# Three x tiles loaded by two DMA queues at once, and parameter loads moved behind ScalarE's table load

## The chip, the cores and the metric

The kernel runs on one core of a Trainium2 chip. The metric is device time in microseconds (us) of one execution.

Engine names in the profile: PE is TensorE (matmul), PEld its weight loads, DVE is VectorE, ACT is ScalarE, POOL is GpSimd, SP is SyncE. A "q" behind a name (SPq, ACTq) is the engine's sequencer; a row such as "SPq ... DMA_DIRECT2D" is the time in which that sequencer *issues* a DMA, not the time in which the data move. PE's results land in a memory called PSUM (`ps`), which the kernel uses in banks.

## The reference, cut to what matters

The input x has 2048 tokens of 1024 features. It is normalised, and three terms are added.

```python
xn = layernorm(x)                       # per token, over 1024 features
return x + A_ref(xn, ...) + B_ref(xn, w1, b1, w2)
# A_ref: a diagonal complex recurrence over the tokens, with projections B (in) and C (out)
# B_ref: (xn @ w1 + b1) -> h * tanh(softplus(h)) -> @ w2, with 3584 hidden features
```

Only the opening matters: before the first real matmul can run, a tile of x must arrive, be normalised and be transposed, and the first columns of w1 must be there.

## The kernel before

Tokens are worked in four blocks of 512, each of four tiles of 128 tokens. The steady part is matmuls end to end. The opening, which the change touches, loads the four x tiles of block 0, the first seven slots of a weight ring and four small parameter vectors. Cuts are marked `# ...`.

```python
for h in range(2):                                   # x tile 0, two column halves, 128 rows x 1 KB
    SP.dma(lambda e, h=h: e.dma_start(xx[:, 0, 0, h * 512:(h + 1) * 512], A_x[0, 0:P, h * 512:(h + 1) * 512]),
           DmaSem(nc, "d_x00_%d" % h), writes=[b_xx[0][0].parts[h]])
for q in (1, 3):
    load_x(SP, 0, q)                                 # x tiles 1 and 3, 128 rows x 2 KB
for src, r0, n in ((A_log_dt, 2 * NJ, NJ), (A_Lambda_im, NJ, NJ), (A_Lambda_re, 0, NJ),
                   (B_b1, 3 * NJ, NF)):              # 8, 8, 8 and 28 rows of 256 B
    AC.dma(lambda e, src=src, r0=r0, n=n: e.dma_start(
        st[r0:r0 + n, :], src.rearrange("(j p) -> j p", p=P)), s_st, writes=[b_st])
# ...
for i in range(NRING):                               # weight slots, 512 KB each
    ring_load()                                      # on SP
    if i == 0:
        load_x(SP, 0, 2)
# ...
keep_busy(36)                                        # filler matmuls, ahead of real work
aop(lambda e: e.activation(rs[:, :, 3], ..., AF.Sqrt), ...)   # its table load comes first on ScalarE
for q in range(2):
    first_sums_v(q, 0); first_sums_v(q, 1)           # VectorE statistics
    first_var_v(q)
    first_sqrt(q)                                    # ScalarE
keep_busy(14, [b_mv[0]])
PE.op(lambda e: e.transpose(ps16(2)[:, 0:NST], st[:, :], ident[0:NST, 0:NST]),   # the parameter block
      reads=[b_st, b_ident], writes=[b_ps[2]])
keep_busy(8, [b_mv[1]])
first_apply(0); first_transpose(0)                   # x tile 0 normalised (VectorE), transposed (PE)
first_apply(1, 2); first_transpose(1)
keep_busy(8)
# ... copies of the transposed tiles to SBUF, then the copy of the parameter block
for f in range(4):
    first_half(f, 0, 0, NK // 2)                     # first w1 matmuls, 256 tokens wide
```

In the profile of before, line L477 is the filler, L393 the transposes of x, L523 the 256-wide w1 matmuls and L665 the full-width (512) ones. In the changed kernel the same lines are L485, L401, L532 and L674.

## Time and profile before

| | before |
|---|---|
| median of 3 runs (lowest to highest) | 621.22 us (621.11 to 621.61) |
| span of the profiled run, granted clock | 620.0 us, 1.0 |
| PE busy | 616.7 us |
| first w1 matmuls / first full-width w1 matmuls start (timeline / chain) | 8.73 / 18.72 us |

First the page's busy times (each with its share of the span and its number of instructions):

```profile
PE 616.7 (99%) x2961; PEld 287.2 (46%) x2961; DVE 462.4 (75%) x677; ACT 247.6 (40%) x161; POOL 50.6 (8%) x47
```

Then the chain of waits of before: the work that ended last, followed back. The columns are start, duration (us) and what it was.

```profile
0.79 2.23 DMA xx<-in_A_x_dram
...
3.04 0.71 DVE stats L351
...
6.52 0.62 PE ps L477 x8
7.14 1.23 PE ps L393 x16
8.38 0.45 PE ps L477 x8
8.82 3.24 PE ps L523 x28
...
13.39 5.33 PE ps L523 x48
18.72 39.71 PE ps L665 x184
```

From 6.52 us on the chain is PE to 617.9 us, 0.4 us before the end. Whatever delays the start of the full-width matmuls at 18.72 us delays the end of the kernel by the same amount.

The timeline of before, opening only: start, duration, engine, line, what; in brackets the idle time in front and what ended it.

```profile
0.79 0.88 SPq L291 DMA_DIRECT2D xx<-in_A_x_dram  x2
0.79 0.59 ACTq L297 DMA_DIRECT2D st<-in_A_log_dt_dram  x1
...
1.72 0.92 SPq L287 DMA_DIRECT2D xx<-in_A_x_dram  x2
...
2.68 0.44 SPq L321 DMA_DIRECT2D ring<-in_B_w_dram  x1
3.04 1.50 DVE L351 BATCH_NORM_STATS2 stats<-xx 128x6 f32<-128x512 bf16 x2 [2.06 <-DMA xx<-in_A_x_dram]
...
6.29 0.19 PE L488 MATMUL ps<-ident,st 52*128 52x52 bf16 x1
...
10.57 1.21 PEld L523 LDWEIGHTS ps<-xnT,ring 128*128 128x128 bf16 x12 [0.21 <-DMA ring<-in_B_w_dram]
```

### The profile page before, as it was taken

What the parts mean: (1) busy time and instruction counts of PE and PEld (TensorE: products, weight loads), DVE (VectorE), ACT (ScalarE), POOL (GpSimd) and SP (SyncE); (2) the same over time, 40 slices, a digit from 0 to 9 for tenths busy, and PEclk for the clock granted to TensorE, in tenths of its full rate; (3) what the DMA queues carried; (4) which work ended last, traced back from release to release, by engine and by line L of the source; (5) the groups of instructions that cost most, each with busy time, mean ns of one, the idle gap of its engine ahead of it and who ended that gap; (6) DMA issues with size and microseconds to landing.
All of it is one profiled execution on the core that took longest, in us unless ns stands there. A gap on an engine that the chain in (4) does not pass through costs nothing.

```text
span 620.0 us, 7386 instructions
## 1 busy us (share of the span) xinstructions
PE 616.7 (99%) x2961; PEld 287.2 (46%) x2961; DVE 462.4 (75%) x677; ACT 247.6 (40%) x161; POOL 50.6 (8%) x47
## 2 busy tenths in 40 slices
PE   9999999999999999999999999999999999999998
PEld 7544444444444444444444444444444444444444
DVE  7897999999467599998147659999624856999603
ACT  5689996440079940000008992000001999000000
POOL 1998000000100000000010000000000000000000
PEclk9999999999999999999999999999999999999999
DMA  8999956840364301783054430276203542033001
GB/s 282 255 294 248 220 111 190 218 136 0 124 204 147 135 1 36 205 197 107 17 187 135 150 122 1 85 204 174 82 35 104 169 167 69 1 122 117 1 0 69
DMA packets 95804, 79.41 MB, mean 128 GB/s; under 512 B 48922, under 2 KB 78234, under 8 KB 95770
## 3 DMA queue, kind: packets, MB, share of 16 engines
q1 hardware_dynamic: 92272, 71.64, 42.1%
q10 hardware_dynamic: 2538, 4.14, 1.8%
q0 software_dynamic: 960, 3.15, 1.6%
q8 instruction: 24, 0.39, 0.3%
q14 instruction: 10, 0.08, 0.0%
HBM read 63.19 MB, written 4.19 MB: 109 GB/s over the span
## 4 chain that ended last, share of the span: by engine, by line
PE 99%; DVE 1%; DMA 0%; issue 0%; DVEq 0%
PE ps L744 49%; PE ps L665 30%; PE ps L686 18%; PE ps L523 1%; DVE stats L351 0%; DMA xx<-in_A_x_dram 0%; PE ps L393 0%; PE ps L758 0%; PE ps L477 0%; DVE xx L812 0%; DVE mv L356 0%; DVE rs L377 0%; DVEq L131 0%
## 5 line engine op out<-in xcount | busy, mean ns | idle before, releaser
L744 PE MATMUL ps<-ring,act 128*128 128x512 bf16 x896 | 194.0, 379 | 0.0
L665 PE MATMUL ps<-xnT,ring 128*128 128x512 bf16 x856 | 185.4, 379 | 0.0
L644 ACT ACTIVATE act<-hb 128x3584 bf16<-128x3584 bf16 x16 | 50.9, 3183 | 224.1 <-DVE hb L673 224.0
L744 PEld LDWEIGHTS ps<-ring,act 128*128 128x128 bf16 x896 | 87.7, 98 | 105.7
L665 PEld LDWEIGHTS ps<-xnT,ring 128*128 128x128 bf16 x856 | 83.7, 98 | 100.8
L673 DVE TENSOR_SCALAR hb<-ps,par 128x512 bf16<-128x512 f32 x112 | 82.4, 747 | 56.0 <-PE ps L665 54.8
L686 PE MATMUL ps<-xnT,BT 128*128 128x512 bf16 x512 | 111.2, 379 | 0.0
L744 PE MATMUL ps<-CT,hT 128*128 128x512 bf16 x506 | 109.9, 379 | 0.0
L691 DVE TENSOR_TENSOR mt<-ps,tab 128x1024 bf16<-128x1024 f32 x64 | 75.4, 1219 | 17.5 <-PE ps L686 16.6
L686 PEld LDWEIGHTS ps<-xnT,BT 128*128 128x128 bf16 x512 | 50.1, 98 | 60.4
L744 PEld LDWEIGHTS ps<-CT,hT 128*128 128x128 bf16 x506 | 49.5, 98 | 59.7
L709 DVE TENSOR_TENSOR_SCAN hT<-cs,qi,hT 128x512 bf16<-128x512 f32 x48 | 58.9, 1269 | 0.0
L789 DVE TENSOR_TENSOR xx<-ps,xx 128x1024 bf16<-128x1024 f32 (+1 forms) x16 | 18.8, 1190 | 46.0 <-PE ps L744 45.9
L645 ACT ACTIVATE act<-act 128x3584 bf16<-128x3584 bf16 x16 | 51.0, 3190 | 0.2
L646 ACT ACTIVATE act<-act 128x3584 bf16<-128x3584 bf16 x16 | 51.0, 3190 | 0.2
L714 DVE TENSOR_TENSOR mt<-hT,tab 128x1024 bf16<-128x1024 bf16 x64 | 41.4, 688 | 1.1
L651 DVE TENSOR_TENSOR act<-act,hb 128x3584 bf16<-128x3584 bf16 x16 | 32.3, 2017 | 1.3 <-ACT act L646 1.3
L287 POOL DMA_DIRECT2D xx<-in_A_x_dram x12 | 6.7, 559 | 253.2 <-DVE xx L789 247.9
L620 ACT ACTIVATE ct<-CT,cs 128x512 f32<-128x512 bf16 x16 | 11.5, 720 | 26.7 <-DVE CT L622 25.9
L645 ACT ACT_TABLE_LOAD x16 | 20.5, 1283 | 0.3
L646 ACT ACT_TABLE_LOAD x16 | 20.5, 1283 | 0.3
L709 DVE TENSOR_TENSOR_SCAN hT<-cs,hT 128x512 bf16<-128x512 f32 x16 | 18.7, 1209 | 0.0
(86 smaller groups left out, 276.7 us busy)
## 6 DMA issues: line engine op xcount, KB each, us to landing
ring<-in_B_w_dram SPq DMA_DIRECT2D x112, 512.0 KB, 4.1
out_dram<-xx ACTq DMA_DIRECT2D x15, 256.0 KB, 2.1
xx<-in_A_x_dram POOLq DMA_DIRECT2D x12, 256.0 KB, 3.5
xx<-in_A_x_dram SPq DMA_DIRECT2D x3, 256.0 KB, 3.7
xx<-in_A_x_dram SPq DMA_DIRECT2D x2, 128.0 KB, 2.2
dsk<-in_A_Dskip_dram SPq DMA_DIRECT2D x1, 256.0 KB, 8.2
xnT<-xn SPq DMA_TRANSPOSE x12, 4.6
BT<-in_A_B_re_dram SPq DMA_TRANSPOSE x8, 6.2
```

The source lines that it names most:

```text
L644: aop(lambda e: e.activation(a, hs, AF.Exp), reads=[b_hb[g % 2]], writes=[b_act[g]])
L645: aop(lambda e: e.activation(a, a, AF.Ln, bias=1.0), reads=[b_act[g]], writes=[b_act[g]])
L646: aop(lambda e: e.activation(a, a, AF.Tanh), reads=[b_act[g]], writes=[b_act[g]])
L651: vop(lambda e: e.tensor_tensor(a, a, hs, op=ALU.mult), reads=[b_act[g], b_hb[g % 2]], writes=[b_act[g]])
L665: PE.mm(lambda e, k=k, w=w: e.matmul(ps[:, bank, :], lhsT=w, rhs=xnT[:, k, :], start=k == 0, stop=k == NK - 1), reads=[b_ring[s]] + b_xnT, ...
L673: vop(lambda e: e.tensor_scalar(hb[:, hs, :], ps[:, bank, :], b1(f), None, op0=ALU.add), reads=[b_ps[bank], b_par], writes=[b_hbf[hs]])
L686: PE.mm(lambda e, j=j, ci=ci, k=k, bank=bank: e.matmul(ps[:, bank + ci, :], lhsT=BT[:, ci, j, k, :], rhs=xnT[:, k, :], start=k == 0, stop= ...
L691: vop(lambda e, s=s, u=u, j=j: e.tensor_tensor(mt[:, s, :, :], u, tab[:, s, j, :].unsqueeze(1).to_broadcast([P, 2, TB]), op=ALU.mult), rea ...
L709: vop(lambda e, ci=ci, init=init: e.tensor_tensor_scan(out=hT[:, ci, j, :], data0=cj("r", j).to_broadcast([P, TB]), data1=hT[:, ci, j, :], ...
L714: vop(lambda e, s=s: e.tensor_tensor(mt[:, s, :, :], hT[:, :, j, :], tab[:, s, j, :].unsqueeze(1).to_broadcast([P, 2, TB]), op=ALU.mult), ...
L744: PE.mm(lambda e: e.matmul(ps[:, u, :], lhsT=lhsT, rhs=rhs, start=st_, stop=last), reads=reads, writes=[b_ps[u]], first=st_, last=last)
L789: vop(lambda e: e.tensor_tensor(xr, src, xr, op=ALU.add), reads=b_ps[bank:bank + n] + [b_x], writes=[b_x])
```

## The change

The intent: the halves of x tiles 0, 1 and 3 are issued by SyncE and ScalarE at the same time, 64 tokens each, so that x is out sooner; ScalarE's parameter loads make room for them and go behind its table load; PE takes the parameter block later, since the parameters come later. The core of the diff:

```diff
+    def load_both(q, lo, hi, sem, bufs):
+        for n, queue in enumerate((SP, AC)):
+            p0 = n * (P // 2)
+            queue.dma(lambda e, p0=p0: e.dma_start(xx[p0:p0 + P // 2, 0, q, lo:hi],
+                                                   A_x[0, q * P + p0:q * P + p0 + P // 2, lo:hi]), sem, writes=bufs)
+
     for h in range(2):
-        SP.dma(lambda e, h=h: e.dma_start(xx[:, 0, 0, h * 512:(h + 1) * 512], A_x[0, 0:P, h * 512:(h + 1) * 512]),
-               DmaSem(nc, "d_x00_%d" % h), writes=[b_xx[0][0].parts[h]])
+        load_both(0, h * 512, h * 512 + 512, DmaSem(nc, "d_x00_%d" % h, nper=2), [b_xx[0][0].parts[h]])
     for q in (1, 3):
-        load_x(SP, 0, q)
-    for src, r0, n in (... the four parameters ...):
-        AC.dma(...)
+        load_both(q, 0, D, DmaSem(nc, "d_x0%d_2" % q, nper=2), [b_xx[0][q]])
+
+    def load_parameters():
+        for src, r0, n in (... the four parameters ...):
+            AC.dma(...)
 # ...
     aop(lambda e: e.activation(rs[:, :, 3], ..., AF.Sqrt), ...)
+    load_parameters()
 # ...
     keep_busy(14, [b_mv[0]])
-    PE.op(lambda e: e.transpose(ps16(2)[:, 0:NST], st[:, :], ...), ...)
     keep_busy(8, [b_mv[1]])
     first_apply(0)
     first_transpose(0)
     first_apply(1, 2)
     first_transpose(1)
+    PE.op(lambda e: e.transpose(ps16(2)[:, 0:NST], st[:, :], ...), ...)
     keep_busy(8)
```

More of the change, by code (lines that the diff above doesn't have):

```diff
@@ L288, in load_x @@
                   s_xx[i][q] if blk else s_x0[q], writes=[b_xx[i][q]])
+    def load_both(q, lo, hi, sem, bufs):
[3 more added lines that the diff above has]
+                                                   A_x[0, q * P + p0:q * P + p0 + P // 2, lo:hi]), sem, writes=bufs)
     for h in range(2):
-        SP.dma(lambda e, h=h: e.dma_start(xx[:, 0, 0, h * 512:(h + 1) * 512], A_x[0, 0:P, h * 512:(h + 1) * 512]),
-               DmaSem(nc, "d_x00_%d" % h), writes=[b_xx[0][0].parts[h]])
+        load_both(0, h * 512, h * 512 + 512, DmaSem(nc, "d_x00_%d" % h, nper=2), [b_xx[0][0].parts[h]])
     for q in (1, 3):
-        load_x(SP, 0, q)
-    for src, r0, n in ((A_log_dt, 2 * NJ, NJ), (A_Lambda_im, NJ, NJ), (A_Lambda_re, 0, NJ),
-                       (B_b1, 3 * NJ, NF)):
-        AC.dma(lambda e, src=src, r0=r0, n=n: e.dma_start(
-            st[r0:r0 + n, :], src.rearrange("(j p) -> j p", p=P)), s_st, writes=[b_st])
+        load_both(q, 0, D, DmaSem(nc, "d_x0%d_2" % q, nper=2), [b_xx[0][q]])
+    def load_parameters():
+        for src, r0, n in ((A_log_dt, 2 * NJ, NJ), (A_Lambda_im, NJ, NJ), (A_Lambda_re, 0, NJ),
+                           (B_b1, 3 * NJ, NF)):
+            AC.dma(lambda e, src=src, r0=r0, n=n: e.dma_start(
+                st[r0:r0 + n, :], src.rearrange("(j p) -> j p", p=P)), s_st, writes=[b_st])
     items = []
@@ L487, in build_kernel @@
     keep_busy(14, [b_mv[0]])
-    PE.op(lambda e: e.transpose(ps16(2)[:, 0:NST], st[:, :], ident[0:NST, 0:NST]),
-          reads=[b_st, b_ident], writes=[b_ps[2]])
     keep_busy(8, [b_mv[1]])
@@ L494, in build_kernel @@
     first_transpose(1)
+    PE.op(lambda e: e.transpose(ps16(2)[:, 0:NST], st[:, :], ident[0:NST, 0:NST]),
+          reads=[b_st, b_ident], writes=[b_ps[2]])
     keep_busy(8)
```

## The prediction

> **What bounds the kernel now.** TensorE. The page gives PE 616.7 of 620.0 us busy, at full clock; the chain of waits is unbroken PE work from 6.52 us to 617.9 us. From 18.72 us on (the first full-width w1 matmuls) the change touches nothing: it can gain or lose only what moves that start.
>
> **The opening, read from the timeline and the chain.** The two halves of x tile 0 are issued at 0.79 and 1.26 us (0.41 us each on SyncE) and take 2.2 and 2.1 us to land. VectorE starts its statistics at 3.04 us and is busy until 6.46; tile 1 (issued 1.72, 3.1 us to landing) arrives at about 4.8, just when VectorE wants it. The transposes start at 7.13, the first w1 matmuls at 8.73. Two limits hide behind it: the weight load at 10.57 waited 0.21 us for the second w1 slot, and VectorE 0.34 us for x tile 2 until 9.05. Both are late in one saturated stream: the DMA share is 0.75 to 1.4 from 2.5 us on.
>
> **What the change does.**
> - The x0, x1, x3 bytes are the same and run on the same DMA engines. The Trainium skill ("DMA: Bandwidth & Descriptors", Rules for kernel authors) says that two transfers to disjoint partition halves share the engines and aren't worth it, and that a second issuing engine saves issue time only. The saturated stream fits.
> - Issue time: 128 rows cost 0.41 to 0.50 us, 8 rows 0.29 to 0.32 us; I estimate 0.35 us for 64 rows. SyncE reaches the first weight load about 0.3 us sooner. But ScalarE's first issue took 0.59 us, twice its later ones (0.29), so its half of x0 is probably out at 1.4 us, against 1.2 us for the same columns today. I expect x0 to land 0.2 us sooner to 0.2 us later. There is a dip to 152 GB/s at 3.0 to 3.5 us that a second queue may fill, worth up to 0.2 us for tile 1 and everything behind.
> - ScalarE: four x issues end near 2.6 us (parameters ended at 2.40), table load 1.28 us, then four parameter issues of 0.3 us: free at about 5.4 not 3.94. The first square root, at 4.82 now, moves to about 5.4. VectorE reads it only at 6.38: hidden.
> - Parameters should land at about 8 us (now before 6.28). PE now needs them after the transposes of tile 1, at about 8.2, ahead of the first w1 matmuls. Tight.
>
> **Sum.** Gain 0 to 0.4 us from earlier x and weights, loss 0 to 0.5 us from late parameters and the transposed block moved onto the path (0.06 to 0.19 us). I predict 621.0 us, 8 in 10 between 620.2 and 622.1. Chance of faster by over 2% 0.005, within 2% 0.99, slower 0.005.
>
> **What would show it.** The start of the first w1 matmuls (8.73 now) and of the full-width ones (18.72 now, predicted 18.3 to 18.9); x0's landing near 3.0; the second w1 slot's landing; ScalarE's first issue again near 0.6 us; PE's wait for the parameter tile under 0.5 us.
>
> **What would make it wrong.** SyncE's weight issues take 5.6 us for five from 3.71 us: held back. If ScalarE's parameter issues are too, the square roots and everything behind slip by 1 to 2 us. Or parameters land after 9 us and PE stands. Or both queues together fill the stream sooner than I think, for a gain of 0.5 us or more.

## More of the kernel before

SyncE needs 1.85 us for its four x issues, and the first weight slot is issued at 2.68 us. The parameter block is transposed at 6.29 us without a wait: the parameters were there (the raw trace has the last of them landed at 4.84 us).

## The result, and the profile after

| | before | after |
|---|---|---|
| median of 6 runs (lowest to highest) | 621.29 us (621.11 to 621.61) | 623.72 us (622.41 to 624.28) |
| span of the profiled run, granted clock | 620.0 us, 1.0 | 622.4 us, 1.0 |
| PE busy | 616.7 us | 616.7 us |
| first full-width w1 matmuls | 18.72 us | 21.15 us |

The ratio is 1.0036 with a 95% interval of 1.0023 to 1.0049. Ratios here are the mean time of one kernel's runs over that of the other's of the same rounds, so not quite the ratio of the medians that are quoted. The change is slower, clear of noise, and lies 1.6 us above the predicted range.

The chain of waits after the change, same columns as before:

```profile
0.80 0.57 ACTq L294
...
5.06 5.59 DMA st<-in_B_b_dram
10.64 0.05 issue
10.69 0.20 PE ps L502
10.88 0.55 PE ps L485 x8
11.44 3.06 PE ps L532 x28
...
15.82 5.33 PE ps L532 x48
21.15 39.71 PE ps L674 x184
```

The chain no longer runs through the landing of x and VectorE. It runs through ScalarE's four x issues, which end at 3.59 us, and the last parameter load, issued at 5.06 us and landed 5.59 us later. The shift of the full-width matmuls, 21.15 - 18.72 = 2.43 us, is the whole difference of the medians (623.72 - 621.29 = 2.43 us), and of the two profiled runs too (623.86 - 621.43).

The timeline after the change shows both new facts:

```profile
0.79 2.48 SPq L294 DMA_DIRECT2D xx<-in_A_x_dram  x4
0.80 2.79 ACTq L294 DMA_DIRECT2D xx<-in_A_x_dram  x4
...
3.31 0.59 SPq L329 DMA_DIRECT2D ring<-in_B_w_dram  x1
3.34 1.50 DVE L359 BATCH_NORM_STATS2 stats<-xx 128x6 f32<-128x512 bf16 x2 [2.35 <-DMA xx<-in_A_x_dram]
...
3.69 0.67 ACTq L305 DMA_DIRECT2D st<-in_A_log_dt_dram  x1
...
5.06 0.33 ACTq L305 DMA_DIRECT2D st<-in_B_b_dram  x1
...
10.69 0.20 PE L502 MATMUL ps<-ident,st 52*128 52x52 bf16 x1 [1.88 <-DMA st<-in_B_b_dram]
```

First, four half issues take SyncE 2.48 us, where four whole ones took 1.85: the weight slot goes out at 3.31 us, not 2.68, and VectorE can start on x tile 0 at 3.34 us, not 3.04. Second, PE stands still for 1.88 us in front of the parameter block. VectorE stands with it: the block's copy sits ahead of the statistics of x tile 2, which began at 11.05 us, not 9.05.

The windows of 2 to 6 us (length, then busy time and number of instructions of PE, PEld, DVE, ACT, POOL; granted clock; mean busy share of the DMA engines; GB/s), before:

```profile
2.00:6.00 4.00, 3.85 (x40) 3.61 (x39) 2.77 (x5) 1.79 (x3) 0.84 (x2) 1.00 0.92 254
```

and after:

```profile
2.00:6.00 4.00, 3.85 (x39) 3.61 (x38) 2.33 (x5) 1.79 (x3) 0.85 (x2) 1.00 0.70 200
```

The DMA engines moved *less* in this stretch: 200 instead of 254 GB/s. Their busy share fell with it (0.70 against 0.92), so they did not work more slowly, they had less to do: x and weights were issued later. In 4 us that is about 0.2 MB (54 GB/s times 4 us), nearly all of it x and weights that come later.

### The profile page after: what moved, and what is told of

It reads as the page before. It is cut to its first block, busy times and chain, and to the rows that moved or that the text cites. A ratio compares the mean times of both kernels' runs of the same rounds, so it can differ in the third digit from the quotient of the medians.

```text
span 622.4 us, 7391 instructions
## 1 busy us (share of the span) xinstructions
PE 616.7 (99%) x2961; PEld 287.5 (46%) x2961; DVE 462.5 (74%) x677; ACT 247.7 (40%) x161; POOL 50.7 (8%) x47
## 4 chain that ended last, share of the span: by engine, by line
PE 98%; DMA 1%; ACTq 1%; ACT 0%; DVE 0%; issue 0%
PE ps L753 49%; PE ps L674 30%; PE ps L695 18%; PE ps L532 1%; DMA st<-in_B_b_dram 1%; ACTq L294 0%; PE ps L767 0%; PE ps L401 0%; ACT L489 0%; ACTq L305 0%; PE ps L485 0%; DVE xx L821 0%; PE ps L502 0%; ACT rs L489 0%
```

## The experiments

The open questions: how much of the 2.43 us is the parameters' late arrival, how much the split of x; why do 13 KB of parameters take 5.6 us to land; and why does issuing on two queues take longer. For the parameters there were three theories. Theory 1: DMAs issued by SyncE and ScalarE are served in order of issue, so the parameters stand behind earlier x and weights. Theory 2: they stand behind ScalarE's own x halves in its own queue. Theory 3: the DMA engines are loaded with the weight stream, and a small load amid it is late whoever issues it.

Each run below was correct. "Over before" is the difference of medians to the kernel before, run on the same chip in the same job. The column "full-width" is the start of the full-width w1 matmuls in the chain of that run's profile (before: 18.72). It stands for one profiled run each, and a thousandth of the time is 0.62 us, so most intervals reach some 0.8 us to either side.

| run | what | over before, us | ratio, 95% interval | full-width, us |
|---|---|---|---|---|
| the change | | +2.43 | 1.0036 (1.0023 to 1.0049) | 21.15 |
| e1 | parameters and block moved, x as before | -0.06 | 1.0003 (0.9988 to 1.0017) | 18.77 |
| e2 | as e1, parameters held to 3.4 us | +2.20 | 1.0042 (1.0027 to 1.0057) | 20.84 |
| e3 | the change, parameters by GpSimd | +3.41 | 1.0058 (1.0043 to 1.0074) | 23.74 |
| e4 | the change, block taken later | +0.66 | 1.0011 (0.9994 to 1.0027) | 21.13 |
| e11 | e4 again, five rounds | +0.95 | 1.0016 (1.0002 to 1.0029) | 19.57 |
| e5 | row halves all on SyncE | +3.00 | 1.0054 (1.0038 to 1.0069) | 21.73 |
| e6 | the change, only x tile 0 split | +0.47 | 1.0007 (0.9993 to 1.002) | 19.13 |
| e7 | the change, later weights held | +3.96 | 1.0073 (1.0058 to 1.0088) | 22.64 |
| e9 | the change, cut by columns | +0.77 | 1.0014 (1.0001 to 1.0026) | 20.05 |
| e10 | e9, block taken later | +0.50 | 1.0008 (0.9995 to 1.002) | 19.26 |
| e8 | another opening | +0.20 | 1.001 (0.9997 to 1.0022) | 19.61 |

The profiles of e3, e4, e8 and e9 fell on runs well above their medians (626.29, 623.79, 622.31 and 622.69 us), so the last column says too much there. All four runs of e5 had a granted clock of 0.995 to 0.997, so its time contains a clock loss (see there).

### e1: the parameter move alone

```diff
 # before, with:
-    AC.dma(...)  x4, the parameters, ahead of everything on ScalarE
     aop(... AF.Sqrt ...)
+    load_parameters()
 # and the parameter block's transpose after first_transpose(1), as in the change
```

> x loaded as before; only the parameter loads moved behind the table load, and the transposed block as in the change. All theories: ScalarE has nothing before them, so they are issued by about 2.3 us and landed long before 8.2 us; PE does not wait for the parameter tile; first w1 matmuls at 8.7 to 8.9 us; total within 0.3 us of before. If the moved block itself cost much, it would be 0.3 us or more slower.

Measured: no wait for the parameter block, and the full-width matmuls at 18.77 us. The parameters were issued from 1.77 to 3.41 us, not by 2.3 us as expected, and landed at 6.95 us (raw trace), still before PE wanted them. So neither the table load in front of them nor the moved block shows a cost by itself (the chain moved by 0.05 us; the interval of the times reaches from -0.7 to +1.1 us). The place behind the table load is not what makes them late.

### e2: the parameters late, with no x on ScalarE

```diff
 # e1, with the parameters waiting for the second half of x tile 0
-    load_parameters()
+    load_parameters(AC, [b_xx[0][0].parts[1]])
```

> x loaded as before, ScalarE issues no x at all, but the parameters are held until the second half of x tile 0 is in (about 3.4 us), so they are issued from 3.4 to 4.8 us, amid SyncE's weight loads, much as in the change. Theory 1 (loads issued by SyncE and ScalarE are served nearly in order of issue, so the parameters stand behind the x and weights issued before them) and theory 3 (the DMA engines are full, so anything is late): landing 4 to 6 us after the last issue, PE waits 0.7 to 2 us, 0.7 to 1.8 us slower than before. Theory 2 (they are late because ScalarE's own queue still holds its x halves): landing about 2.5 us after issue, no wait, within 0.3 us of before.

The chain of e2:

```profile
4.65 5.63 DMA st<-in_B_b_dram
10.28 0.05 issue
10.33 0.19 PE ps L495
```

The last parameter load took 5.63 us, as in the change (5.59), although ScalarE had issued nothing else. Theory 2 falls. PE waited 1.4 us; with +2.20 us the loss was a little larger than the 1.8 expected, partly because x tile 1 also came later (VectorE waited 0.58 us for it).

### e3: the parameters issued by GpSimd

```diff
 # the change, with
-    load_parameters()
+    load_parameters(PO, [b_xx[0][0].parts[0]])     # on GpSimd, from 3.57 us
```

> The change with the parameter loads issued by GpSimd at about 3.3 us, once the first half of x tile 0 is in. Theory 1 (order of issue on the path that SyncE and ScalarE share): GpSimd's loads go round it and land by about 8.3 us; PE waits under 0.3 us; first w1 matmuls at about 9.2 us; 0.3 to 0.7 us slower than before. Theory 3 (engines full): they land at 10 us or later, PE waits 1.5 us or more, about as slow as the change (2.4 us over before).

The chain of e3:

```profile
5.32 6.19 DMA st<-in_B_b_dram
11.51 0.05 issue
11.56 0.20 PE ps L502
11.75 0.55 PE ps L485 x8
12.30 4.72 PE ps L532 x28
```

A third queue, whose loads nothing in front of them on that queue can hold back, was later still: 6.19 us. Theory 1, an order of issue on the path that SyncE and ScalarE share, falls; theory 3 stands. The profile lists GpSimd's queue as another kind (software_dynamic), but that kind is not slow as such: in the kernel before, GpSimd's 256 KB x loads land after 3.5 us at the median, SyncE's after 3.7. That it is slower for small loads alone no run excludes. (An order kept by the DMA engines themselves, whoever issues, would be a form of theory 3.)

This run is worse than the change for a second reason. PE had been idle for 2.74 us, and its clock was halved for a while, as the windows of e3 show (columns as above; the clock is the number before the last two):

```profile
12.00:13.00 1.00, 1.00 (x12) 0.84 (x10) 0.97 (x2) 0.00 (x0) 0.00 (x0) 0.74 1.10 362
13.00:14.00 1.00, 1.00 (x7) 0.69 (x6) 0.60 (x3) 0.39 (x2) 0.00 (x0) 0.50 1.11 349
```

The 28 first w1 matmuls took 4.72 us in the chain instead of 3.06. In the change itself, after 1.88 us of idle PE, the clock stayed at 1.00 and the same matmuls took 3.06 us (3.24 before), so none of its 2.43 us is this.

### e4 and e11: the change without the wait

```diff
 # the change, with
-    PE.op(... e.transpose(ps16(2) ...))           # after first_transpose(1)
-    vop(... tensor_copy(par, ps16(2) ...))
+    PE.op(... e.transpose(ps16(5) ...))           # after first_transpose(3), another PSUM bank
+    vop(... tensor_copy(par, ps16(5) ...))
     first_half(4, 0)
```

> The change with the parameter tile's transpose and its copy put after the transposes of x tile 3, into another PSUM bank, so that PE no longer meets the late parameters. If the parameters are 1.9 us of the 2.4 us and the later x the other 0.4 to 0.5: no PE wait for the parameter tile, first w1 matmuls at 9.1 to 9.3 us, 0.3 to 0.7 us slower than before. Rival: the parameters are the whole loss: within 0.15 us of before.

> e4 again, with more rounds, since its interval held both zero and the predicted 0.3 to 0.7 us. If the row split by itself costs: 0.3 to 1.0 us slower than before, interval above zero. If only the late parameters cost: within 0.2 us.

The first try was not clear (+0.66 us, interval across zero), so it was run again with more rounds: +0.95 us, interval above zero (0.1 to 1.8 us). Its five runs lie between 622.23 and 622.54 us. The chain of e11:

```profile
2.30 3.23 DMA xx<-in_A_x_dram
...
5.55 0.70 DVE stats L359
...
7.28 0.62 PE ps L485 x8
...
19.57 4.48 PE ps L674 x20
```

The chain is back on x and VectorE, but later: statistics of x tile 1 begin at 5.55 us, against 4.80 before. This splits the loss in two: about 0.9 us stays when PE no longer waits for the parameters, and the remaining 1.5 us (2.43 - 0.95) is what the parameters added. It is less than PE's 1.88 us of idle time, since without that wait PE meets the later x instead.

### e6: fewer loads in front

```diff
     for q in (1, 3):
-        load_both(q, 0, D, DmaSem(nc, "d_x0%d_2" % q, nper=2), [b_xx[0][q]])
+        load_x(SP, 0, q)
```

> The change with only x tile 0 split over two queues, tiles 1 and 3 whole on SyncE. ScalarE has two x issues before the parameters, so they go out from about 2.3 to 3.9 us instead of 3.7 to 5.4. If lateness grows with the load in front: they land at 7 to 8.5 us, PE waits under 0.4 us, total 0 to 0.6 us slower than before. If the two-queue issue is slow by itself, x tile 0 still lands at about 3.3 us, not 3.0.

The parameters went out from 2.37 to 4.13 us, 1.3 us earlier than in the change. The last of them landed 4.1 us after its issue, at 7.91 us (raw trace), where the change took 5.59. PE did not wait for them at all (the block ran at 8.67 us). X tile 0 was in at 3.26 us. As expected on both counts: lateness goes with the load in front, and the row split alone delays x.

### e7: less weight stream behind

```diff
 # the change; weight slots 2 to 7 wait on SyncE for the parameter tile
-        SP.dma(lambda e: e.dma_start(dst, src), s_ring[s], writes=[b_ring[s]])
+        SP.dma(lambda e: e.dma_start(dst, src), s_ring[s], reads=after, writes=[b_ring[s]])
```

> The change with the second and later weight loads held on SyncE until the parameters are in. Theory 3 (lateness is the load of the weight stream on the DMA engines): the parameters, issued at the same 3.7 to 5.4 us, land by about 8.6 us, 3.5 us or less after the last issue instead of 5.6, and PE's wait for them falls under 0.5 us. If 256 B loads are slow by themselves, or behind x and the first weight slot, they land at 10 us or later as in the change. The weights come later, so the total says little: about the change's or worse.

The chain of e7:

```profile
5.05 4.25 DMA st<-in_B_b_dram
```

The last parameter load took 4.25 us (5.05 to 9.30) instead of 5.59, and PE waited 0.60 us instead of 1.88. Better, but not the 3.5 us expected: the x tiles, the first weight slot and x tile 2 were still under way. So the later weights account for some 1.3 us of the lateness and the rest lies in what was already there, or in the small loads themselves; this run can't part those two. (Its total, +3.96 us, says nothing of the parameters: PE then waited for the weights that were held.)

The kept traces can part them. They record the start, duration and size of every DMA packet (the piece that a DMA engine moves at one go) and the time of every semaphore update; no view above prints these. Read directly from the trace files, they give for the last parameter load, 28 rows of 256 B (e3's packets are cut in another way and are left out):

| run | issued, us | landed after, us | data moved between its issue and the start of its last packet, KB |
|---|---|---|---|
| e5 | 2.12 | 1.79 | 143 |
| before | 2.08 | 2.76 | 594 |
| e1 | 3.05 | 3.90 | 1097 |
| e6 | 3.81 | 4.10 | 1038 |
| e7 | 5.05 | 4.25 | 863 |
| e2 | 4.65 | 5.63 | 1531 |
| the change | 5.06 | 5.59 | 1567 |
| e9 | 3.52 | 5.97 | 1528 |

A parameter packet lasted 18 ns at most in every one of these runs. What grew is the time before the packets started: the last one began at 4.41 us in the kernel before and at 10.07 us in the change. With little else under way (e5, whose x is issued slowly) the same load landed after 1.79 us. So the small loads are not slow by themselves. The lateness is waiting ahead of the packets, while the DMA engines move other data. What holds the packets there, the records don't say.

### e5, e9, e10, e12: what an issue costs, and what two queues buy

```diff
 # e5: row halves, one queue; parameters and block as before
-        for n, queue in enumerate((SP, AC)):
+        for n, queue in enumerate((SP, SP)):
```

> The row halves of x tiles 0, 1 and 3 all issued by SyncE, one after the other; parameters and the transposed block as before. If a 64-row issue costs little more than half of a 128-row one, it takes 0.3 to 0.35 us here (0.58 in the change), and the eight end at about 3.3 us, as the change's four pairs did: then the second queue bought no issue time, since two queues together issue no faster than one. If a 64-row issue costs 0.4 us or more alone, the eight end after 4 us and the second queue did buy time. Parameters early, no PE wait for them. Total 0.2 to 0.8 us slower than before through the later weights.

The times of e5's eight 64-row issues on SyncE (min/median/max in ns, then first and last start in us):

```profile
L294 SPq DMA_DIRECT2D xx<-in_A_x_dram x8: 574/596/677, 0.8 to 5.3; - x8
```

The second alternative held, by more than I had thought: the eight issues took 5.13 us, over 0.6 us each, on one queue. So the slow issues of the change are not two queues in each other's way; a 64-row issue is dear by itself. Against this form the second queue did save issue time, as the change meant it to (2.48 us for SyncE's four). Against whole tiles it didn't. The total was a miss: +3.00 us, not 0.2 to 0.8. The x tiles came late (statistics of x tile 1 began at 6.79 us, 4.80 before), PE idled, and the granted clock was 0.50 from 8.4 to 11.8 us.

e12 measured the cost alone, at the very end of the kernel when nothing else runs.

```diff
 # before, with, after the last store:
+    for q, r0, n, lo, hi in ((0, 0, 128, 0, 1024), (1, 0, 64, 0, 1024), ... ):
+        SP.dma(lambda e, ...: e.dma_start(xx[r0:r0 + n, 0, q, lo:hi], A_x[0, r0:r0 + n, lo:hi]), s_probe, ...)
```

> The kernel before with nine loads of known shapes issued by SyncE alone at the very end, when nothing else runs: 128, 64, 32, 16 and 8 rows of 2 KB, 128 and 64 rows of 1 KB. If an issue costs a base plus so much per row: 64 rows take 0.35 us, between 8 rows (0.29) and 128 rows (0.43). If 64 rows have a dear form of their own, as e5 suggests: about 0.6 us alone, more than 128 rows. Correct result; total about 6 us longer.

The probe's issues of 128, 64 and 32 rows of 2 KB (duration in ns, three times the same since each line is one issue, then its start in us):

```profile
L870 SPq DMA_DIRECT2D xx<-in_A_x_dram x1: 447/447/447, 617.9 to 617.9; - x1
L870 SPq DMA_DIRECT2D xx<-in_A_x_dram x1: 569/569/569, 618.4 to 618.4; - x1
L870 SPq DMA_DIRECT2D xx<-in_A_x_dram x1: 586/586/586, 619.7 to 619.7; - x1
```

A second issue of 64 rows took 587 ns and one of 32 rows 583. The others: 16 rows 412 ns, 8 rows 364 ns; with 1 KB rows, 128 rows 356 ns and 64 rows 471 ns. An issue of half the rows costs 0.12 us *more* than one of all 128. My estimate of 0.35 us, a straight line between 8 and 128 rows, was wrong in kind. Why 32 and 64 rows are dear is not shown.

e9 then cut the tiles by columns, which keeps 128 rows per issue.

```diff
-            queue.dma(lambda e, p0=p0: e.dma_start(xx[p0:p0 + P // 2, 0, q, lo:hi], ...), sem, ...)
+            queue.dma(lambda e, d=d: e.dma_start(xx[:, 0, q, d], A_x[0, q * P:(q + 1) * P, d]), sems[h], ...)
```

> The change with each of x tiles 0, 1 and 3 cut by columns (128 rows of 1 KB per queue) instead of by rows (64 rows). e5 showed a 64-row issue at 0.64 us with one queue alone, so the rows, not the second queue, may be what is dear. If so: 0.41 to 0.45 us per issue on SyncE (three instead of four issues before the first weight load, which goes out near 2.1 us, not 3.3); x tile 0's first half at about 3.0 us; parameters out by 3.8 us and landed by about 8.2; PE waits under 0.4 us; within 0.3 us of before, over 1.5 us faster than the change. If two queues slow each other, the issues take 0.55 us or more and x lands after 3.3 us.

The issues of e9 on the two queues:

```profile
L294 ACTq DMA_DIRECT2D xx<-in_A_x_dram x3: 410/453/468, 0.8 to 1.7; - x3
L294 SPq DMA_DIRECT2D xx<-in_A_x_dram x3: 404/412/424, 0.8 to 1.7; - x3
```

As expected, the issues are short again, and SyncE reaches the first weight slot at 2.18 us, half a microsecond before the kernel before does. VectorE's start in e9:

```profile
3.38 1.50 DVE L357 BATCH_NORM_STATS2 stats<-xx 128x6 f32<-128x512 bf16 x2 [2.39 <-DMA xx<-in_A_x_dram]
```

So VectorE could start on x tile 0's first half only at 3.38 us, *later* than before (3.04), though it was issued at the same 0.79 us by the same engine in the same form. What is new beside it is the other half, issued at the same moment on the other queue. Before, the first half was issued 0.47 us ahead of the second and came first. The packet records show what happened: the first half's packets began at 1.81 us (1.83 before), but the last of its 128 began at 2.83 us instead of 2.47, and 90 packets of the other half had begun by then. The two halves took DMA time from each other. The parameters were late here too, 5.97 us after their last issue at 3.52 us, and PE waited 0.92 us in the profiled run. Expected was a landing by about 8.2 us; it was 9.49. This is a miss, and so is the total, +0.77 us where 0.3 at most was expected. As much data moved while the parameters waited as in the change (table above), although they were issued 1.5 us earlier.

> e9 with the parameter block's transpose and copy after the transposes of x tile 3, as in e4: the possible winner. If the parameters still cost in e9: 0.2 to 0.5 us faster than e9 and 0.1 to 0.4 us faster than before. If x and the weights limit: equal to e9 within 0.2 us.

e10, with the block taken later (diff as in e4), is at +0.50 us (interval across zero): 0.27 us better than e9, as expected, but not better than before, where 0.1 to 0.4 us was expected. With the best form of split tried and no wait for parameters left, no gain from two queues shows here.

### e8: a version meant to beat both

```diff
 # e1, with the parameter block taken later as in e4, and
-    keep_busy(8)
+    keep_busy(3)
     first_mean_a(3)
```

> Not the change: x as before on SyncE, table load first and parameters behind it, the transposed block and its copy put after the transposes of x tile 3, and 3 instead of 8 filler matmuls ahead of the first w1 matmuls. In e1 the first w1 matmuls started at 8.84 us, held by block and filler, while the copies they read were done at about 8.5. Expected: they start at 8.5 to 8.6 us, full-width ones at about 18.4 instead of 18.72; total 0.1 to 0.4 us faster than before. If the second weight slot or x tile 2 limits: no difference.

A miss. The median was 0.20 us above before, interval across zero. In the profiled run x tile 1 came late (VectorE waited for it until 5.67 us), the first w1 matmuls started at 9.60 us, and the filler that was cut had no part in it. In e1, with the same loads in the same order, x tile 1 was in by 4.81 us: one landing can differ by 0.9 us from run to run, so a single profile, that of e11 too, says less than the times. No version tried beats the kernel before.

## Why the prediction was wrong

- **Right: what bounds the kernel.** The full-width start moved by 2.43 us and the time by 2.43 us; nothing after it changed (PE busy is 616.7 us in both). It was also right that the split would buy no bandwidth. The Trainium skill ("DMA: Bandwidth & Descriptors", Rules for kernel authors) advises against two transfers to disjoint partition halves since they share the engines; the trace agrees that nothing was gained (200 instead of 254 GB/s from 2 to 6 us), though the fall itself comes from the later issues, as the busy share shows.
- **Wrong, the step that failed first: "Parameters should land at about 8 us ... Tight", and PE's wait "under 0.5 us".** They landed at 10.64 us and PE waited 1.88 us. The prediction let them issue until 5.4 us and allowed some 2.6 us from there, close to the 2.4 us that they took in the kernel before (2.40 to 4.84 us). The end of their issue came out right (5.39 us), but by luck: ScalarE's x issues ended 1 us later than predicted (3.59 against 2.6 us), and the parameter issues did not wait for the table load of 1.28 us to end, as the sum had it, but began 0.07 us after its start. The step that failed is the 2.6 us: amid the weight stream it was 5.25 us. e2 and e3 show that it takes about as long from another queue and with nothing else on ScalarE; e6 and e7 show that it shortens with less load; the packet records (e7) show that the time is waiting before the packets start. The prediction named this outcome ("parameters land after 9 us and PE stands") but kept it out of the range. This term is about 1.5 us of the 2.43.
- **Wrong: "Gain 0 to 0.4 us from earlier x and weights".** It was a loss of about 0.9 us (e11: +0.95). The step underneath is "I estimate 0.35 us for 64 rows": a 64-row issue took 0.57 to 0.60 us on SyncE. So SyncE reached the weights 0.63 us later, not 0.3 us sooner, and x tile 0 landed 0.30 us later, outside the 0.2 us that I allowed: its first packets began at 2.14 us (SyncE) and 2.41 us (ScalarE), not 1.83. The dip at 3.0 to 3.5 us that a second queue "may fill" rose from 152 to 197 GB/s, but the half microseconds on both sides of it fell, and the stretch as a whole moved less.
- **Right for the wrong reason: "ScalarE's first issue again near 0.6 us".** It took 0.57 us, but so did SyncE's: it is the 64-row form. In e9 none of ScalarE's x issues took over 0.47 us, its first included. The 0.59 us seen before belongs to the first parameter load, which took 0.67 us in the change too, as ScalarE's fifth issue.
- **Right, with the same luck: the square roots.** The first one moved from 4.82 to 5.44 us (predicted about 5.4) and nothing waited for it; its time rests on the same sum of issues. ScalarE's parameter issues were not held back (0.29 to 0.33 us after the first).

Still open: what keeps the packets of a handful of 256 B rows waiting for 4 to 6 us in a loaded stream. The same page ("Latency and other measured facts") says that memory latency rises under load and that lighter load makes the fixed cost smaller. e7 agrees in direction (4.25 against 5.59 us), but the parameters' packets ran no longer (18 ns at most in both) and only started later; whether memory latency has a part in that, no record shows. The split of the 2.43 us into 1.5 and 0.9 is good to some 0.2 us at best: it sets runs of different jobs against each other, and the runs of most kernels here scatter by that much or more. The recorded intervals of the two are wider still, about 0.8 us to either side.

## What to carry to other kernels

Cost a small load that something waits for by its landing under the traffic of that moment, not by its landing on idle DMA engines: here the same 7 KB load took 1.8 us (e5) and 2.8 us (before) early, and 5.6 us amid the stream from ScalarE and 6.2 from GpSimd. If such loads can go out before the stream starts, leave them there, and place their consumer where the late landing does no harm. Measure the issue time of the very shape that you mean to use: half the rows were dearer to issue than all of them, and a second queue did not bring the piece that is wanted first any sooner, in either cut.

## What the Trainium skill lacked or had wrong

- "DMA: Bandwidth & Descriptors", Issuing engines are not separate DMA queues, says that initiating on several engines saves the sequencer's time only. For one and the same form the runs agree: eight half-row issues took SyncE 5.13 us alone (e5), its four in the change 2.48 us. What the page lacks is that the form can eat the saving: four whole issues took 1.85 us. No page has the issue cost by rows: 128, 64, 32, 16 and 8 rows of 2 KB took 447, 569, 586, 412 and 364 ns (e12).
- The same page, Queues, rings and completion order, says that each DMA engine takes turns between the queues at packet granularity. One might conclude that a small load on an otherwise idle queue gets through a busy stream quickly. It landed 5.6 us (ScalarE, e2) and 6.2 us (GpSimd, e3) after issue. No page gives the landing time of a small load beside a saturated stream.
- "TensorE: Matmul & The Clock Gate", Part 1, puts the return to half clock at one idle window of about 3.4 us. In e3 the granted clock fell to 0.50 after 2.74 us of idle PE; in e5 it was 0.50 from 8.4 to 11.8 us, with idle gaps of 0.91 and 1.46 us and 1 us of work between them; in the change, 1.88 us did not lower it. The 3.41 us just before the fall were not idle throughout: PE was busy for 0.91 us of them in e3 and 1.17 us in e5. The page gives no share of work that is enough.
